# RWKV-style attention, routed experts and a dense layer on one core: loads of 48 rows, and the attention's pieces from one written list

## The chip, the core and the metric

The kernel runs on one core of a Trainium2 chip. The metric is the device time of one execution in microseconds (us), as a median of several runs; lower is better. The core has five engines with queues of their own: PE (matrix products, with the weight loads PEld as a second row of the profile), DVE (vector), ACT (scalar), POOL (GpSimd) and SP, which here only issues transfers. Transfers run on 16 DMA engines that all queues share.

## The reference

Three layers follow each other. The first is a linear attention with a state of 40x40 for each of 4x8 heads, over 768 steps; the second sends each of the 3072 tokens to one of 8 experts; the third is a dense layer with an exponential activation.

```python
for t in range(S):                      # S = 768, per (batch, head)
    y[:, :, t] = np.einsum('bhd,bhde->bhe', rt, state)
    Sa = np.einsum('bhde,bhe->bhd', state, at)
    state = state * wt[:, :, None, :] - np.einsum('bhd,bhe->bhde', Sa, bt) + np.einsum('bhd,bhe->bhde', vt, kt)
...
logits = x @ w_gate; expert_idx = np.argmax(logits, axis=1)      # x: 3072 x 320
h = np.maximum(disp @ w1, 0.0); y = h @ w2                       # 8 experts, 320 -> 1024 -> 320
out[i] = gate_w[i] * y[expert_idx[i], pos[i]]
...
h = x @ w_in; g = np.where(h > 0, h, np.exp(np.minimum(h, 0)) - 1); return g @ w_out   # 320 -> 2048 -> 320
```

## The kernel before

**Units.** The 768 steps are cut into 12 chunks of 64. A unit is one chunk of 16 of the 32 heads, so there are 24 units, u = 0 to 23; units of one parity follow each other through the state, so the work is two interleaved recurrences. A unit's 16 heads lie as 8 pairs on two halves of the partitions: rows 0 to 39 and 64 to 103 hold the 40 channels.

**Steps of a unit.** Each step is a generator whose `yield` stands where another engine takes over, and has a letter. `e`/`E` loads the unit's decays, a, k and b (from `in_e`, two transfers of 40 rows x 2058 words; `e` on SP in two halves for the first ten units, `E` on the ACT queue later), `d` loads r and v (`in_d`, two transfers of 40 rows), `v` loads v by token. `p` makes running decays and scales a, k, b on DVE (L243 to L255). `a` copies a on ACT, `c` is the score product on PE (L277), its eviction on ACT and the store of the scores to a DRAM scratch `dab`; `m` masks them (L295), `k` transposes k and b (L304, L306). `l` brings a piece of `dab` back with one small system a partition; `i` solves those systems on POOL by 31 steps of two instructions (L351, L353), for a group of units at once: groups 0 and 1 are units 0, 1 and 2, 3, and groups 2 to 6 are four units each. `o` stores the solution (`dx`), `t` loads it for one unit, `f`/`g` join small inverses to one of 64 (PE L433 and L444, DVE L426). Then the recurrence: `r` (PE L459), `u` (L469, ACT L471), `w` (L479), `s` (L494, DVE L503, L504), `h`, and beside it the outputs `q` (L525, DVE L530), `z` and `y` (L539, L552, DVE L556) and `x` (L562, ACT L567, DVE L569), which gives token rows and their logits. `b`, `j` and `D` route the rows and scatter them into the expert buffers (POOL L610). `V` are pieces of DVE work that split the dense layer's weights ahead of time, and a further generator loads and splits the first expert's weights.

**What sets the order.** Every engine runs its instructions in the order in which the program gives them out. That order is a list of step names: each name runs its step to its next `yield`. Before, the first part is written out as text (`ORDER`), up to the first pieces of the slot of unit 5, and the rest is made by `slot(k)` for k = 5 to 24 from one pattern. A name stands in the list as often as its step has pieces; `q15.1` is the second half of `q` of unit 15.

**After the attention** the expert blocks and then the dense layer run on PE, with everything else beside it.

Of the kernel before, what the change touches and what calls it, by code (L numbers as in the profile page):

```python
# [33 lines left out]
ORDER = """
se1 sa0 se0 se0 v1 sc0 e0.0 sv se1 e0.1 sd p0 sw p0 e1.0 sw a0 p0 v0 p1 sa1 sx a0 p1 lw sz st1 e2.0 c0.0 a1
p2 p2 a1 c0.0 e1.1 sr1 Z7 c0.1 p1 e3.0 c0.1 k0.0 k0.1 c0.1 c1.0 e2.1 a2 a2 c1.0 p3 c1.1 k1.1 k1.0 c1.1 k1.0 e4.0 d1 k1.1
c1.1 e3.1 m0.0 l0 m0.1 k0.1 p2 p3 a3 l1 a3 p4 p4 p3 m1.1 c2.1 e5.0 k2.1 c2.0 c2.1 m1.0 r0 c2.0 k2.0 k0.0 a4 m2.1 a4 p5
st0 k2.0 k3.1 sc1 c3.0 c2.1 c3.1 ss1 k3.0 e4.1 m2.0 p4 r0 r1 c4.0 i0 e6.0 k3.0 n0 k3.1 m3.0 k4.1 p5 n1 o0 c3.1 p6
c3.0 e5.1 a5 a5 c3.1 m3.1 k2.1 r1 e7.0 l2 p5 k4.1 c4.1 k4.0 m4.1 e6.1 c4.0 c5.1 k5.1 l3 p6 k5.0 c5.0 c4.1 p7 c4.1 p6 a6
m5.0 a6 v2 v3 p7 c5.0 t1 m4.0 t0 c6.1 m6.1 c5.1 k4.0 f1 k6.1 c5.1 k6.0 k6.1 m5.1 sr0 a7 i1 c6.0 f1 f0 a7 o1 e7.1 e8.0 f1 f0  # L40
k5.0 p7 c6.1 f0 f1 f1 p8 c6.0 d0 e9.0 f0 k5.1 c7.1 f0 f1 f1 c6.1 c7.0 f0 f0 e8.1 c7.1 g1 c7.0 g0 p8 m7.0 a8 ss0 p8 m7.1
g0 k7.1 l5 l4 g1 k7.0 k7.1 g0 k8.0 g0 c7.1 l6 p9 e9.1 g1 a8 u0 m6.0 p9 k6.0 k8.1 u0 g1 l7 c8.0 k7.0 m8.0 c8.1 n2 t2 e10
w0 a9 p9 f2 n3 k8.1 a9 q0.0 w0 q0.1 q0.1 w0 i2 u1 u1 f2 q0.0 c8.0 f2 p10 k9.1 c9.1 f2 c8.1 c9.0 m8.1 k8.0 Z2 c8.1 f2 w0
Z4 p10 t3 f2 s0 k9.1 p10 c9.1 c9.0 w1 w1 k9.0 y0 f2 i2 k9.0 g2 s0 w1 e11 s0 c9.1 f3 k10.1 Z3 r2 a10 w1 a10 f3 k10.1 m9.0
f3 y0 m9.1 k10.0 p11 Z0 r2 c10.0 q1.0 q1.0 c10.1 x0 f3 p11 h2 q1.1 s1 f3 g2 a11 k10.0 m10.1 i2 f3 c10.0 g2 q1.1 c10.1 h2
e12 v4 p11 f3 s1 c10.1 x0 y1 y1 d2 g3 p12 a11 s1 k11.1 c11.0 x1 g3 r3 Z6 c11.0 g2 g3 p12 k11.1 h3 x1 m11.0 a12 Z5 p12 x0 r3
u2 a12 c11.1 c12.0 u2 g3 w2 d3 c11.1 w2 k11.0 w2 x1 k12.1 h3 q2.0 q2.1 Z1 b0 w2 c11.1 c12.1 u3 c12.1 m10.0 m11.1 s2 j0
o2 u3 w3 k11.0 q2.1 q3.1 c12.0 e13 z2 q2.0 s2 w3 y2 s2 l11 j0 l10 y2 t4 m12.0 m12.1 r4 v5 l9 g4 d4 w3 k12.1 r4 p13 D0
h4 x2 l8 g4 c12.1 k12.0 D1 h4 t5 q3.0 p13 w3 g4 g4 g4 s3 u4 x2 a13 l12 s3 z3 q3.0 u4 w4 w4 a13 q3.1 p13 i3 w4 g5 h5 y3
d5 x2 w4 y3 s3 s4 i3 k12.0 e14 t6 s4 s4 h5 v6  # L50
"""
FIRST = [f for f, n in GROUPS if f > 6]
AHEAD = (17, 19, 20, 21, 22, 23)

CV0, CVN = 17, 7


def slot(k):
    L = []
    a = lambda x: L.extend(x.split())  # L60
    live = k < NU

    nx, up = k + 1, k + (8 if k < 7 else 9)
    ups = up < NU
    pair = k - 3 if k % 2 else None
    work = {f - 6 + i: (g, i) for g, (f, n) in enumerate(GROUPS) for i in range(4) if f > 8}
    work[5] = (3, 3)
    w = work.get(k)
    if live: a(f"r{k} r{k}")
    if ups and k != 7: a(f"c{up}.0")  # L70
    if FU <= k < NU: a(f"g{k} g{k}")
    more = ups and up + 1 < NU
    if ups and k != 7: a(f"m{up}.0 c{up}.0")
    if more and k != 7: a(f"p{up+1}")
    a(f"x{k-2} x{k-2} x{k-2}")
    if k == NU: a(f"b{NU-2}.1")
    if FU <= k < NU: a(f"g{k} g{k}")
    if w and w[1]:
        a(f"i{w[0]}")
        if w[1] == 3: a(f"o{w[0]}")  # L80
    if k % 2 == 0: a(f"D{k-3}")
    second = f"c{up}.1 m{up}.1 c{up}.1 c{up}.1 p{up+1} l{up}"
    if ups: a(second if k != 7 else f"a{up} a{up} c{up}.0 m{up}.0 c{up}.0 p{up+1}")
    if k + 2 < NU: a(f"v{k+2}")
    V = (lambda: a("V")) if CV0 <= k < NU else (lambda: None)

    if nx in FIRST: a(f"t{nx}")
    a(f"q{k-1}.0 q{k-1}.0")
    V()
    if w and not w[1] and k != 6: a(f"i{w[0]}")  # L90
    if live: a(f"u{k} u{k}")
    if k == 7: a(second)
    if more: a(f"p{up+1}")
    a(f"q{k-1}.1 q{k-1}.1")
    V()
    if pair is not None: a(f"b{pair}")
    if ups:
        a(f"k{up}.0 k{up}.0 k{up}.1 k{up}.1")
    if FU <= nx < NU and nx not in FIRST: a(f"g{nx}")
    if live and k < 22: a(f"w{k} w{k} w{k} w{k}")  # L100
    if up + 2 < NU: a(f"E{up+2}")
    if more: a(f"a{up+1} a{up+1}")
    a(f"z{k-1}")
    if nx < NU: a(f"h{nx} h{nx}")
    if nx < NU: a(f"d{nx}")
    if k + 2 < NU and k + 2 not in FIRST: a(f"t{k+2}")
    if live and k < 22: a(f"s{k} s{k} s{k}")
    if k == NU: a(f"j{NU-2}.1 j{NU-2}.1 D{NU-2}")
    a(f"y{k-1} y{k-1}")
    if nx in FIRST: a(f"g{nx}")  # L110
    V()
    if pair is not None: a(f"j{pair} j{pair} D{pair}")
    if k == 6:
        up += 1
        a(f"c{up}.0 m{up}.0 c{up}.0 c{up}.1 m{up}.1 c{up}.1 c{up}.1 p{up+1} l{up} i{w[0]}")
        a(f"k{up}.0 k{up}.0 k{up}.1 k{up}.1 E{up+2} p{up+1} p{up+1}")
    return " ".join(L)


def attention(tc, nc, e_in, v_tok, d_in, wg, disp, xt, cst, ring, early, early_w, cv, cap):  # L120
# [548 lines left out]
    for k in range(KR, NU + 1):
        for key in slot(k).split():  # L670
            go(key)
        for _ in range(AHEAD.count(k)):
            next(early, None)
        if k == 8:
            zero_x()
# [813 lines left out]
```

## Time and profile before

| | |
|---|---|
| median of 3 runs | 1049.46 us (1043.61 to 1050.21) |
| time of the profiled execution | 1050.7 us |
| its span, first to last instruction | 1049.0 us |
| mean granted clock of PE | 0.946 |
| busy: PE, DVE, POOL, ACT | 963.1, 726.2, 614.4, 514.5 us |

A time on a row counts from the span's start. "Idle before, releaser" in brackets is the time for which the engine stood still ahead of the row, and what ended it. The granted clock (PEclk) is a share of full speed; in the trace it stands at 0.5 or at 1.0, and a stretch shows the mean. The DMA share is the mean busy share of the 16 DMA engines.

### The profile page before, as it was taken

How to read it: one execution, taken by the hardware profiler on the slowest of the kernel's cores; microseconds unless marked ns; L12 is line 12 of the kernel's file. 1: busy time of each engine (PE TensorE's matmuls, PEld its weight loads, DVE VectorE, ACT ScalarE, POOL GpSimd, SP SyncE). 2: the span in 40 equal slices, each digit the busy share in tenths (PEclk: the TensorE clock that was granted, in tenths of full speed). 3: DMA queues.
4: the chain of work that ended last, by engine and by line, in shares of the span. 5: the costliest groups of instructions: out<-in, count | busy, mean ns of one | idle time of the engine just before them, and what ended most of it. 6: DMA issues, size and time to landing. Idle time of an engine off the chain costs nothing.

```text
span 1049.0 us, 25349 instructions
## 1 busy us (share of the span) xinstructions
PE 963.1 (92%) x9995; PEld 868.3 (83%) x9995; DVE 726.2 (69%) x1287; ACT 514.5 (49%) x1011; POOL 614.4 (59%) x926
## 2 busy tenths in 40 slices
PE   4869988898899999989999999999999999999993
PEld 4858877798888888778988888889889988998893
DVE  8955857888674567649888963676667667676761
ACT  4646544556363334254445456464555555554551
POOL 4767839899898803377777776744333334333342
PEclk9866989899899889999999999999999999999997
DMA  6768776667555585376877764501001010100000
GB/s 169 163 175 185 179 138 117 150 136 140 129 118 115 126 199 117 120 215 202 258 225 213 216 201 149 199 23 26 26 1 45 7 26 26 26 26 1 26 1 28
DMA packets 180984, 121.67 MB, mean 116 GB/s; under 512 B 105792, under 2 KB 166872, under 8 KB 179224
## 3 DMA queue, kind: packets, MB, share of 16 engines
q1 hardware_dynamic: 176788, 102.89, 39.5%
q0 software_dynamic: 3168, 11.14, 3.0%
q10 hardware_dynamic: 900, 5.93, 2.2%
q8 instruction: 81, 1.33, 0.6%
q14 instruction: 47, 0.39, 0.1%
HBM read 86.87 MB, written 33.05 MB: 114 GB/s over the span
## 4 chain that ended last, share of the span: by engine, by line
PE 41%; DVE 7%; issue 3%; DMA 3%; ACT 2%; POOL 1%; SPq 0%; POOLq 0%; ACTq 0%; DVEq 0%
PE ph L968 21%; PE po L994 5%; PE po L993 5%; PE po L992 5%; DVE L L1098 1%; DMA w<-E 1%; ACT X L1091 1%; DVE E L859 1%; DVE N L864 1%; PE po L1037 1%; PE po L1039 1%; DMA xt<-Y 1%; DMA ring<-in_w_dram 1%; PE po L1038 1%; PE po L1033 1%
## 5 line engine op out<-in xcount | busy, mean ns | idle before, releaser
L780 POOL TENSOR_TENSOR ring<-ring,ring 128x64 fp32r<-128x64 f32 (+2 forms) x320 | 197.0, 656 | 83.9 <-ACT ring L775 83.9
L1112 POOL TENSOR_TENSOR L<-E,H 128x512 fp32r<-128x512 f32 x66 | 94.3, 1429 | 166.6 <-ACT H L1111 154.4
L968 PE MATMUL ph<-XH,ring 128*128 128x512 f32 (+1 forms) x640 | 170.7, 388 | 0.9 <-ACT XH L952 0.5
L1105 ACT ACTIVATE E<-N 128x512 f32<-128x512 f32 x96 | 60.8, 633 | 155.1 <-POOL L L1112 78.0
L968 PEld LDWEIGHTS ph<-XH,ring 128*128 128x128 f32 x640 | 115.7, 189 | 15.3 <-ACT XH L952 0.9
L353 POOL TENSOR_TENSOR X<-X,ring 128x60 f32<-128x60 f32 (+19 forms) x170 | 115.6, 680 | 13.3
L994 PE MATMUL po<-ring,L 128*128 128x320 f32 x384 | 119.4, 311 | 1.5 <-POOL L L1112 1.5
L992 PE MATMUL po<-ring,H 128*128 128x320 f32 x384 | 118.5, 309 | 0.4 <-ACT H L1111 0.4
L993 PE MATMUL po<-ring,H 128*128 128x320 f32 x384 | 118.5, 309 | 0.0
L968 PE MATMUL ph<-XS,ring 128*128 128x512 f32 (+1 forms) x320 | 97.1, 384 | 0.0
L968 PE MATMUL ph<-XL,ring 128*128 128x512 f32 (+1 forms) x320 | 96.9, 384 | 0.0
L351 POOL TENSOR_TENSOR ring<-X,ring 128x60 f32<-128x60 f32 (+19 forms) x108 | 73.8, 683 | 37.2 <-DMA ring<-dab 16.6
L1104 DVE TENSOR_SCALAR N<-ph 128x512 f32<-128x512 f32 x96 | 65.7, 685 | 33.2 <-PE ph L968 33.0
L1109 DVE SCALAR_TENSOR_TENSOR M<-E,M 128x512 f32<-128x512 f32 x96 | 72.6, 756 | 14.5 <-ACT M L1106 14.5
L992 PEld LDWEIGHTS po<-ring,H 128*128 128x128 f32 x384 | 72.1, 188 | 4.8 <-ACT H L1111 0.6
L993 PEld LDWEIGHTS po<-ring,H 128*128 128x128 f32 x384 | 72.1, 188 | 4.3
L994 PEld LDWEIGHTS po<-ring,L 128*128 128x128 f32 x384 | 72.2, 188 | 2.0 <-POOL L L1112 2.0
L1110 DVE SCALAR_TENSOR_TENSOR E<-ph,M 128x512 f32<-128x512 f32 x96 | 66.4, 692 | 7.8
L968 PEld LDWEIGHTS ph<-XL,ring 128*128 128x128 f32 x320 | 60.9, 190 | 11.1
L968 PEld LDWEIGHTS ph<-XS,ring 128*128 128x128 f32 x320 | 60.1, 188 | 10.8 <-DVE XS L953 0.4
L775 ACT CAST ring<-ring 128x704 fp32r<-128x704 f32 x80 | 61.4, 779 | 13.7 <-PE po L1039 6.8
L1111 ACT CAST H<-E 128x512 fp32r<-128x512 f32 x96 | 59.0, 614 | 11.0 <-DVE E L1110 7.8
(238 smaller groups left out, 2162.9 us busy)
## 6 DMA issues: line engine op xcount, KB each, us to landing
ring<-in_w_dram SPq DMA_DIRECT2D x16, 640.0 KB
ring<-in_w_dram SPq DMA_DIRECT2D x32, 256.0 KB
RVU<-in_d_in_dram SPq DMA_DIRECT2D x48, 160.0 KB
dab<-AB SPq DMA_DIRECT2D x24, 256.0 KB
ring<-in_e_in_dram ACTq DMA_DIRECT2D x18, 321.6 KB
ring<-w SPq DMA_DIRECT2D x4, 1408.0 KB
disp<-ring SPq DMA_DIRECT2D x8, 575.8 KB
...
```

The lines of the kernel that those rows point to most:

```text
L351: nc.gpsimd.tensor_tensor(tv, X[:, 0:n, s:s + 1].to_broadcast([128, n, m]), N[:, s:s + 1, s + 1:e].to_broadcast([128, n, m]), op=ALU.mult)
L353: nc.gpsimd.tensor_tensor(X[:, 0:n, s + 1:e], X[:, 0:n, s + 1:e], tv, op=ALU.subtract)
L775: s.nc.scalar.copy(B[:, 0:704], r)
L780: s.nc.gpsimd.tensor_tensor(B[:, to], r[:, q], B[:, q].bitcast(F32), op=ALU.subtract)
L968: nc.tensor.matmul(p, l, r[:, 0:s.T], start=i == 0, stop=i == len(seq) - 1)
L992: nc.tensor.matmul(o, H[:, c], hb, start=f == 0, stop=False)
L993: nc.tensor.matmul(o, H[:, c], lb, start=False, stop=False)
L994: nc.tensor.matmul(o, L[:, c], hb, start=False, stop=f == s.W.nf - 1)
L1104: nc.vector.tensor_scalar(N, p, 0.0, None, op0=ALU.min)
L1109: nc.vector.scalar_tensor_tensor(out=M, in0=E, scalar=1.0, in1=M, op0=ALU.add, op1=ALU.mult)
L1110: nc.vector.scalar_tensor_tensor(out=E, in0=p, scalar=0.0, in1=M, op0=ALU.max, op1=ALU.add)
L1112: eng.tensor_tensor(L, E, H.bitcast(F32), op=ALU.subtract)
```

## The change

Three things change. (1) The loads `e`, `E` and `d` move 48 rows in place of 40: the host pads each half by eight rows (decays of one, the rest zero), which land on partitions 40 to 47 and 104 to 111. (2) `slot` is gone, and one written list gives out all pieces of the 24 units; it holds the same 1335 names as before, and 72 of them stand elsewhere. Two new names are no steps: `A` takes the next piece of the first expert's weights and `X` clears a row of the token buffer, both where the loop did it before. (3) For the last unit alone the logits (L569) are given out ahead of the ACT copy of its token rows.

```diff
@@ load_e
-            eng.dma_start(out=t[64 * hp:64 * hp + 40, c], in_=e_in[u, hp, :, c])
+            eng.dma_start(out=t[64 * hp:64 * hp + 48, c], in_=e_in[u, hp, :, c])
@@ load_d
-            nc.sync.dma_start(out=RVU[u % 2][64 * bp:64 * bp + 40, :, bp:3:2 - bp], in_=d_in[u, bp])
+            nc.sync.dma_start(out=RVU[u % 2][64 * bp:64 * bp + 48, :, bp:3:2 - bp], in_=d_in[u, bp])
@@ x_out
+        logits = lambda: nc.vector.tensor_reduce(cst["lg"][:, u, 1:9], pv[:, :, 80:88].rearrange("p j e -> p e j"), axis=AX.X, op=ALU.add)
+        if u == NU - 1:
+            logits()
         nc.scalar.copy(XO[:, 0:D].rearrange("p (j x) -> p j x", j=4), pv[:, :, 0:80])
         yield
-        nc.vector.tensor_reduce(cst["lg"][:, u, 1:9], pv[:, :, 80:88].rearrange("p j e -> p e j"), axis=AX.X, op=ALU.add)
+        if u < NU - 1:
+            logits()
@@ ORDER
...
+y3 s3 s4 i3 k12.0 e14 s4 s4 h5 v6 r5 r5 c13.0 x3 g5 t6 g5 m13.0 c13.0 p14 x3 x3 c13.1 g5 g5 i3 o3 m13.1 c13.1 c13.1 p14 l13 v7 q4.0 q4.0 u5 u5 p14
...
+h23 V j20 j20 h23 D20 A x22 x22 x22 b22.1 D21 q23.0 q23.0 q23.1 q23.1 z23 y23 y23 j22.1 j22.1 D22
@@ go
+        if key == "A":
+            next(early, None)
+            return
@@ host_layout
+    pad = np.zeros((24, 2, 8, 2058), np.float32)
+    pad[..., 0:520] = 1
+    pad[..., 0:520:65] = 0
...
+    return np.concatenate([out, pad], 2), v_tok, np.concatenate([d_in, np.zeros_like(d_in[:, :, 0:8])], 2)
```

**Place 1: SP, the loads that feed the first solve of four units.** `LM` holds group 2's systems; `dab_556`, `dab_587`, `dab_805` and `dab_904` (`dab_901` in the change) are the scores of units 4, 5, 6 and 7, and `ring_91` is the buffer of the odd units' `e` loads. Before:

```order
L330 DMA LM_106<-dab_587 16x32x32 x2
L330 DMA LM_106<-dab_556 16x32x32 x2
L291 DMA dab_904<-AB 64x1024
L330 DMA LM_106<-dab_805 16x32x32 x2
L230 DMA ring_91<-in_e_in_dram 40x1024 x2
L330 DMA LM_106<-dab_904 16x32x32 x2
L365 DMA TA<-dab_401 64x8x64 x2
```

And with the change:

```order
L286 DMA LM_106<-dab_587 16x32x32 x2
L286 DMA LM_106<-dab_556 16x32x32 x2
L286 DMA LM_106<-dab_805 16x32x32 x2
L247 DMA dab_901<-AB 64x1024
L186 DMA ring_91<-in_e_in_dram 48x1024 x2
L286 DMA LM_106<-dab_901 16x32x32 x2
L321 DMA TA<-dab_500 64x8x64 x2
```

The load of unit 6's systems goes ahead of the store of unit 7's scores; the `e` load stays between that store and the load that reads it back.

**Place 2: PE, the start of the slot of unit 5.** `xp` and `t_...` are the two products of `g`, `x` is the token product of unit 3, `sc` the scores of unit 13. Before:

```order
L459 MATMUL rhs<-VS_138,AM_132 64x40 x16
L277 MATMUL sc<-ring_91 128x128 x4
L433 MATMUL xp<-AB,TA 32x32 x16
L562 MATMUL x<-IW,XT 128x88 x4
L444 MATMUL t_2151<-TT_122,TA 32x32 x16
L277 MATMUL sc<-ring_91 128x128 x4
```

And with the change:

```order
L415 MATMUL rhs<-VS_138,AM_132 64x40 x16
L233 MATMUL sc<-ring_91 128x128 x4
L518 MATMUL x<-IW,XT 128x88 x4
L389 MATMUL xp<-AB,TA 32x32 x16
L233 MATMUL sc<-ring_91 128x128 x4
L400 MATMUL t_2156<-TT_122,TA 32x32 x16
```

The token product now stands ahead of the first product of `g`, and the second half of the scores ahead of its second; unit 6 has the same two moves.

**Place 3: PE, the end of the attention.** `y` and `x` belong to unit 23, `rt` counts the rows of unit 22 and then of unit 23. Before:

```order
L539 MATMUL y<-RVU_120,SD_141 64x128 x8
L597 LDWEIGHTS tri
L597 MATMUL rt<-roh,tri 128x8
L598 LDWEIGHTS ones
L598 MATMUL rt<-ACC,ones 128x8
L552 MATMUL y<-Qs,KB_109 64x64 x16
L562 MATMUL x<-IW,XT 128x88 x4
L634 MATMUL warm<-ring_5566 128x512 x6
```

And with the change:

```order
L495 MATMUL y<-RVU_120,SD_141 64x128 x8
L508 MATMUL y<-Qs,KB_109 64x64 x16
L557 LDWEIGHTS tri
L557 MATMUL rt<-roh,tri 128x8
L558 LDWEIGHTS ones
L558 MATMUL rt<-ACC,ones 128x8
L518 MATMUL x<-IW,XT 128x88 x4
L594 MATMUL warm<-ring_5567 128x512 x6
```

Unit 23's output product stands ahead of the counting of unit 22.

## Rows read from the trace of the kernel before

**Rows 1.** Busy time by stage: stretch, length, engines (instructions), granted clock, DMA.

```profile
0.00:60.00 60.00, 35.20 (x288) 33.86 (x288) 46.84 (x84) 30.61 (x62) 38.61 (x91) 0.90 0.66 164
60.00:143.00 83.00, 72.43 (x1474) 67.26 (x1474) 55.42 (x93) 43.94 (x99) 55.45 (x92) 0.76 0.77 180
143.00:278.00 135.00, 120.64 (x2180) 110.12 (x2180) 103.47 (x185) 72.79 (x158) 113.11 (x160) 0.91 0.67 137
278.00:444.00 166.00, 155.07 (x2985) 140.60 (x2986) 109.58 (x267) 65.18 (x150) 98.17 (x158) 0.93 0.55 128
444.00:1049.00 605.00, 579.78 (x3070) 516.46 (x3068) 410.89 (x662) 301.96 (x542) 309.08 (x428) 0.99 0.31 94
```

**Rows 2.** Waits of PE, 140 to 445 us: total, times, longest.

```profile
PE vu L479 <- ACT RVU L471: 7.8, 5, 4.0
PE xp L433 <- DVE AB L426: 6.3, 2, 3.2
PE sc L277 <- ACT ring L264: 2.7, 1, 2.7
```

**Rows 3.** POOL in order of time: first instruction of solves 0, 2, 3; a store.

```profile
30.18 0.34 POOL L351 TENSOR_TENSOR ring<-X,ring 128x15 f32<-128x15 f32 x1 [16.55 <-DMA ring<-dab]
...
82.56 0.23 POOL L351 TENSOR_TENSOR ring<-X,LM 128x31 f32<-128x31 f32 x1 [11.43 <-DMA TA<-dab]
...
151.89 0.23 POOL L351 TENSOR_TENSOR ring<-X,ring 128x31 f32<-128x31 f32 x1 [12.17 <-DMA dab<-AB]
...
264.06 0.61 POOL L359 DMA_DIRECT2D dx<-X  x1 [0.30 <-POOL X L353]
```

**Rows 4.** The page: ACT's DMA queue (packets, MB, share); its issues (number, size).

```profile
q10 hardware_dynamic: 900, 5.93, 2.2%
...
ring<-in_e_in_dram ACTq DMA_DIRECT2D x18, 321.6 KB
```

**Rows 5.** Who waited for the E loads (us, times).

```profile
  DVE ring L243: 16.0, 11
  DVE ring L255: 4.3, 3
```

**Rows 6.** DVE and SP in order of time, ahead of solve 2.

```profile
64.88 1.25 DVE L255 TENSOR_TENSOR ring<-ring 104x1024 f32<-104x1024 f32 x1 [3.17 <-DMA ring<-in_e_in_dram]
...
72.36 0.50 SPq L291 DMA_DIRECT2D dab<-AB  x1
...
77.10 0.68 SPq L230 DMA_DIRECT2D ring<-in_e_in_dram  x2
77.88 0.86 SPq L330 DMA_DIRECT2D LM<-dab  x2
```

**Rows 7.** SP in order of time, between solves 2 and 3.

```profile
130.10 0.37 SPq L359 DMA_DIRECT2D dx<-X  x1
130.57 0.95 SPq L230 DMA_DIRECT2D ring<-in_e_in_dram  x2
...
134.70 4.59 SPq L379 DMA_DIRECT2D TA<-dx  x1
...
146.79 1.02 SPq L330 DMA_DIRECT2D ring<-dab  x2
```

**Rows 8.** DVE in order of time, unit 12's first use of solve 4.

```profile
277.74 0.70 DVE L426 STREAM_TRANSPOSE AB<-TA 32x512 f32<-32x512 f32 x1 [3.23 <-DMA TA<-dx]
```

**Rows 9.** The end of the attention: DVE, and POOL's last scatter, in order of time.

```profile
440.67 0.19 DVE L569 TENSOR_REDUCE LG<-x 128x8 f32<-128x32 f32 x1 [1.68 <-ACT XO L567]
...
443.57 0.96 POOL L610 DMA_INDIRECT disp<-XO,SLOT  x1 [3.68 <-issue]
```

**Rows 10.** PE in order of time: what moved products take, and the last token product.

```profile
195.72 1.12 PE L562 MATMUL x<-IW,XT 128*128 128x88 f32 x8
...
274.31 1.16 PE L277 MATMUL sc<-ring 128*128 128x128 f32 x8
...
439.05 1.12 PE L562 MATMUL x<-IW,XT 128*128 128x88 f32 x8 [0.79 <-DVE XT L556]
```

More of the change, by code (lines that the diff above doesn't have):

```diff
@@ L39 @@
[L39 to L48, printed above, removed]
@@ L49 @@
-h4 x2 l8 g4 c12.1 k12.0 D1 h4 t5 q3.0 p13 w3 g4 g4 g4 s3 u4 x2 a13 l12 s3 z3 q3.0 u4 w4 w4 a13 q3.1 p13 i3 w4 g5 h5 y3
-d5 x2 w4 y3 s3 s4 i3 k12.0 e14 t6 s4 s4 h5 v6
-"""
[L52 to L117, printed above, removed]
@@ new lines @@
+se1 sa0 se0 se0 v1 sc0 e0.0 sv se1 e0.1 sd p0 sw p0 e1.0 a0 p0 v0 p1 sa1 sx a0 p1 sw lw sz st1 e2.0 c0.0 a1 p2 p2 a1 c0.0 e1.1 sr1 Z7 c0.1 p1 e3.0
+c0.1 k0.0 k0.1 c0.1 e2.1 a2 a2 p3 c1.1 c1.0 c1.0 k1.1 k1.0 c1.1 k1.0 e4.0 d1 k1.1 c1.1 e3.1 m0.0 l0 m0.1 k0.1 p2 p3 a3 l1 a3 p4 p4 p3 m1.1 c2.1 e5.0
+k2.1 c2.0 c2.1 m1.0 r0 c2.0 k2.0 k0.0 a4 m2.1 a4 p5 st0 k2.0 k3.1 sc1 c3.0 c2.1 c3.1 ss1 k3.0 e4.1 m2.0 r1 p4 c4.0 r0 i0 e6.0 k3.0 n0 k3.1 m3.0 p5 n1
+o0 c3.1 p6 c3.0 e5.1 a5 a5 c3.1 m3.1 k2.1 r1 e7.0 l2 p5 k4.1 k4.1 c4.1 k4.0 m4.1 e6.1 c4.0 c5.1 k5.1 l3 p6 k5.0 c5.0 c4.1 p7 c4.1 p6 a6 m5.0 a6 v2 v3
@@ new lines @@
+p17 v9 t8 q6.0 q6.0 u7 u7 c16.1 m16.1 c16.1 c16.1 p17 l16 p17 q6.1 q6.1 b4 k16.0 k16.0 k16.1 k16.1 w7 w7 w7 w7 E18 a17 a17 z6 h8 h8 d8 t9 s7 s7 s7 y6
+y6 g8 j4 j4 D4 r8 r8 c17.0 g8 g8 m17.0 c17.0 p18 x6 x6 x6 g8 g8 i4 D5 c17.1 m17.1 c17.1 c17.1 p18 l17 v10 q7.0 q7.0 u8 u8 p18 q7.1 q7.1 k17.0 k17.0
+k17.1 k17.1 g9 w8 w8 w8 w8 E19 a18 a18 z7 d9 h9 h9 t10 s8 s8 s8 y7 y7 X r9 r9 c18.0 g9 g9 m18.0 c18.0 p19 x7 x7 x7 g9 g9 i4 o4 c18.1 m18.1 c18.1 c18.1
+p19 l18 v11 q8.0 q8.0 u9 u9 p19 q8.1 q8.1 b6 k18.0 k18.0 k18.1 k18.1 g10 w9 w9 z8 w9 w9 E20 a19 a19 h10 h10 d10 t11 s9 s9 s9 y8 y8 j6 j6 D6 r10 r10
@@ new lines @@
+q14.1 q14.1 b12 w15 w15 z14 w15 w15 s15 h16 h16 d16 t17 s15 s15 y14 y14 g16 j12 j12 D12 r16 r16 g16 g16 x14 x14 x14 g16 g16 k23.0 i6 D13 v18 q15.0
+q15.0 u16 u16 q15.1 q15.1 g17 w16 w16 w16 w16 z15 d17 t18 s16 h17 h17 s16 s16 y15 y15 r17 r17 g17 g17 x15 x15 x15 g17 g17 i6 o6 q16.0 q16.0 V V u17
+u17 q16.1 q16.1 b14 g18 v19 w17 w17 w17 w17 z16 h18 h18 d18 t19 s17 s17 s17 y16 y16 V j14 j14 D14 A r18 r18 g18 g18 x16 V x16 x16 g18 g18 D15 v20
+q17.0 q17.0 u18 q17.1 q17.1 V g19 u18 w18 w18 z17 w18 w18 h19 d19 s18 s18 s18 y17 y17 V r19 r19 g19 g19 x17 x17 x17 g19 g19 v21 t20 q18.0 q18.0 V u19
@@ new lines @@
+u19 q18.1 q18.1 V b16 w19 w19 w19 w19 z18 d20 t21 s19 h20 h20 s19 s19 y18 y18 g20 V j16 j16 D16 D17 A r20 r20 g20 g20 x18 x18 x18 h19 g20 g20 v22
+q19.0 q19.0 V V u20 u20 q19.1 q19.1 g21 w20 w20 w20 w20 h21 z19 h21 d21 t22 s20 s20 s20 y19 y19 V V A r21 r21 g21 g21 x19 x19 x19 g21 g21 v23 q20.0
+q20.0 u21 u21 q20.1 q20.1 V b18 g22 w21 w21 w21 w21 z20 h22 h22 d22 t23 s21 s21 s21 y20 y20 V j18 j18 D18 A r22 r22 g22 g22 x20 x20 x20 g22 g22 D19
+q21.0 q21.0 V u22 u22 q21.1 q21.1 V g23 z21 d23 y21 y21 V A r23 r23 g23 g23 x21 x21 x21 g23 g23 q22.0 q22.0 V u23 u23 q22.1 q22.1 V b20 z22 y22 y22
@@ L120, in attention @@
+h23 V j20 j20 h23 D20 A x22 x22 x22 b22.1 D21 q23.0 q23.0 q23.1 q23.1 z23 y23 y23 j22.1 j22.1 D22
+"""
+CVN = 7
 def attention(tc, nc, e_in, v_tok, d_in, wg, disp, xt, cst, ring, early, early_w, cv, cap):
@@ L637, in attention @@
                  n=m_load, t=tt_load, f=t32, g=t64, r=rhs, u=u_solve, w=vu_tr, s=s_update, h=s_tr, q=q_mm, z=y_state, y=y_mm, x=x_out,
-                 b=route, j=route_mm, D=scatter, Z=zero_d, V=lambda: cv.pieces(spare, CVN))
+                 b=route, j=route_mm, D=scatter, Z=zero_d, X=zero_x, V=lambda: cv.pieces(spare, CVN))
     def spare(i, words):
@@ L668, in attention @@
         go(key)
[L669 to L675, printed above, removed]
     for _ in early:
@@ L1449, in d_side @@
         return np.ascontiguousarray(y.transpose(3, 0, 1, 5, 2, 4)).reshape(24, 2, 40, 8, 64)
-    return out, v_tok, np.stack([d_side(r), d_side(v)], 4)
+    pad = np.zeros((24, 2, 8, 2058), np.float32)
+    pad[..., 0:520] = 1
+    pad[..., 0:520:65] = 0
+    d_in = np.stack([d_side(r), d_side(v)], 4)
+    return np.concatenate([out, pad], 2), v_tok, np.concatenate([d_in, np.zeros_like(d_in[:, :, 0:8])], 2)
 def network(tc, nc, e_in, v_tok, d_in, wg, cap, w1, w2, w_in, w_out, out):
```

24 lines of the change are left out of this document (19 added, 5 removed).

## The prediction, made before the result was known

> **What bounds the kernel now.** I read the busy times by stage first. From 444 us on nothing of the change is left: the experts and the dense layer take 605 us, PE is busy for 579.8 of them at a granted clock of 0.99, and no instruction there is moved [rows 1]. So only the attention, 0 to 444 us, can change. Its stages differ. Up to 60 us PE is busy for 35 of 60 us and DVE for 47: the start is a chain of loads, preparation and first scores. From 60 to 143 us PE is busier (72 of 83) but at a mean clock of 0.76, and from 143 to 444 us it is busy for 120.6 of 135 and 155.1 of 166 us at 0.91 and 0.93. The DMA engines are busiest where the start is decided: a mean share of 0.66 and 0.77 up to 143 us, 0.67 and 0.55 after.
>
> Then I read POOL in order of time, because its solves are one long series and each waits for transfers at its start. Solve 0 starts at 30.18 us after 16.55 us of waiting, solve 2 at 82.56 after 11.43, solve 3 at 151.89 after 12.17 [rows 3]. Behind that point POOL hardly stops: solve 4 is stored at 264.06 us, and POOL is busy for 113.1 us of the stretch from 143 to 278, of which 8.9 us lie ahead of solve 3 [rows 1, 3]. At 277.74 us DVE takes up unit 12, the first of solve 4, after 3.23 us of waiting for a load of that solution [rows 8]. So up to unit 12 the pace is that of the solves: what PE alone gains between 143 and 278 us it gives back there, and what lets solves 2 and 3 start earlier is kept. Behind unit 12 PE and the recurrence decide; PE stands still there for 166 - 155.1 = 10.9 us [rows 1].
>
> **The loads of 48 rows.** What they do to a transfer has to be bounded, since no load of 48 rows is in this trace. The ACT queue carries nothing but 18 E loads, two for each of nine units: 900 packets for 18 issues are 50 each, 40 rows and ten more [rows 4]. I read the ten as one closing packet for each DMA engine that takes part: ten engines with four rows each. 48 rows divide into 16 engines with three each. A load would then move a fifth more bytes, but its fullest engine would carry a quarter less, and the ten engines that all E and d loads share would be relieved by a quarter of that traffic.
>
> [...]
>
> What it is worth is read from the waits. DVE waits for E loads 11 times for 16.0 us and three times for 4.3 us [rows 5]; most of these stand where DVE is not the last to arrive, so the total is an upper bound only. The ones on the way to a solve count.
>
> *Ahead of solve 2* the way is: the second half of unit 7's E load, for which DVE waits 3.17 us until 64.88; its scores, stored at 72.36; the load that reads them back, issued at 77.88; solve 2 at 82.56 [rows 3, 6]. The wait of 3.17 us could go wholly or not at all. I take half, 1.5 us, because the load's own travel shrinks by at most a quarter while the queueing behind other loads shrinks with it. For the read-back, 82.56 - 77.88 = 4.7 us, I take 0.5 us of less crowding. Together 2.0 us, between 0 and 4.4 (the whole wait and a quarter of the read-back).
>
> *Ahead of solve 3* there are 151.89 - 130.10 = 21.8 us between the store of solve 2 and the first step of solve 3, nearly all transfers: the store, with a full E load issued 0.5 us behind it, the first load of the result, which holds SP's queue for 4.59 us from 134.70, and behind it in that queue the last scores' load, issued at 146.79, 5.1 us before the solve [rows 3, 7]. A quarter off all of it would be 5.4 us; but most of these transfers use other shapes and only share the engines. I take 1.5 us, between 0 and 5.4.
>
> PE's wait of 2.7 us for an ACT copy of a [rows 2] has an E load behind it, but it lies ahead of unit 12, where solve 4 sets the pace; it only helps PE to keep up. I count 0. The d loads' extra rows cost SP nothing, since the number of issues stays.
>
> **The list.** 72 names stand elsewhere and none is new, so no engine has more work; only who waits changes. At the first place SP gives out the read-back of unit 6 ahead of unit 7's store. Nothing is bought by it: solve 2 needs unit 7's read-back, and that stays behind an E load that holds the queue until 77.10 [rows 6]. At the second place x (1.12 us on PE) goes ahead of g's first product and half of the scores (1.16 us) ahead of its second [rows 10], in the slots of units 5 and 6. That brings scores forward by about a microsecond and puts the unit's inverse back by 2.3. It lies ahead of unit 12; I count 0, between -4.6 (both units, wholly on the recurrence) and +2. For the moves behind unit 12 (pieces of V, of y, of z between the two halves of w) the most that can be filled is the 10.9 us for which PE stands still [rows 1]; the longest named waits of PE, 7.8 us for the eviction of u and 6.3 us for DVE's turn in g [rows 2], have their causes on ACT, DVE and in loads, not in the list's order around them. I take 2.0 us, between -3 and +7.
>
> *The end of the attention* is a plain chain. The last token product starts at 439.05 and takes 1.12 us, so it ends at 440.17; the logits start at 440.67, after waiting for ACT's copy, and the last scatter at 443.57 [rows 9, 10]. Given out first, the logits start 0.5 us earlier, and with the third place's move y no longer waits for the counting of unit 22, some 0.1 us. I take 0.6 us. ACT's copy then waits for the logits, but only the scatter needs it, nearly three microseconds later.
>
> **The sum.** 2.0 + 1.5 + 2.0 + 0.6 = 6.1 us less than the profiled execution's 1050.7 us (span 1049.0 and 1.7 around it): 1044.6 us. That execution was 1.2 us over the median of the runs, 1049.46, so the median after should be near **1043 us**, 0.6% less. Differences under 1% are about what a measurement of this kernel can't tell from no change.
>
> **The rivals.**
> *The loads carry more than I grant them.* If the ten shared engines are what holds up nearly everything before 278 us, the waits for E loads go nearly in full at the places that count and the scores come back faster as well. Price: half of the 20.3 us of DVE waits [rows 5], plus a quarter of the 11.43 and 12.17 us that POOL waits ahead of solves 2 and 3 [rows 3], 5.9 us, plus the list and the end as above, 2.6 us: 10.2 + 5.9 + 2.6 = 18.7 us, about 1031 us. For it speaks the DMA share of 0.77 as a mean over 16 engines: if ten carry more than the rest, those are near full. Against it: POOL would have to start each solve 5 to 10 us earlier, and DVE, busy for 47 of the first 60 us, has little room there.
> *Hidden anyway.* Solve 2's start hangs on SP's order and on PE's clock (0.76 in that stage), not on how long a load travels, and the moves cancel. Then only the end's 0.6 us is left: 1049 us.
> *The recurrence is put back.* The pieces set ahead of g and of w's second half (x and scores in the slots of units 5 and 6, 2.3 us each; z, of about the length of x, 1.1 us, ahead of w's second half in four slots) stand on the way from one state to the next of the same parity. If that way, and not PE's load or the solves, sets a slot's length, each delays all that follows: 4.6 + 4.4 = 9.0 us, and against the loads' 3.5 and the end's 0.6 us the kernel is 4.9 us slower, about 1054 us; if the other moves do the same it reaches 1061. It decides from the point where ACT's and DVE's evictions, not PE, end last in a slot. For it speaks the 7.8 us of PE waiting for u's eviction [rows 2]; against it that PE is busy for 93% of the time behind unit 12.
>
> **How the numbers follow.** The forecast, 3 to 10 us less, has 0.47. The larger gain, 11 to 24 us, has 0.32: the terms' upper ends add to 17.9 us with the end. Hidden anyway (within 3 us of before) has 0.11. The recurrence put back has 0.10, of which half stays within 1% (10.5 us). So faster by over 1% is 0.32, within 1% is 0.63, slower by over 1% is 0.05. The range runs from 1028 (most of the larger gain) to 1054 (the smaller price of the slower case).
>
> **What would show it.** The ACT queue's packets should be 18 x 64 = 1152 in place of 900. Solve 2 should start near 80.5 us and solve 3 near 148; the waits of DVE for E loads should fall below 14 us in total; unit 12's first use should be near 274, the logits' reduction should follow the last token product with no ACT copy between, and the last scatter should start near 437.5. The stretch behind it should still take 605 us. If solve 3 starts below 144 us, the larger gain is at work; if it starts where it did, and the end has moved, the list did it; if the starts have moved and the last scatter has not, the recurrence took the gain back.

## The result and the profile after

The changed kernel takes 1062.72 us (median of 6 runs, 1054.22 to 1067.07) against 1049.84 us of the kernel before beside it: a ratio of 1.013, interval 1.0094 to 1.0166. It is 12.9 us slower; the forecast was 1043. The profiled execution took 1067.07 us, with a span of 1065.4 us, 16.4 us more than before; it is the slowest of the six. Beside it stands a second profile of the same kernel, from the run `after2` below: 1058.39 us, the fastest of another six. Single profiles of one kernel differ by several us, so the readings that carry the argument are given from both.

Lines that were there before have numbers lower by 40 to 46, most by 44 (solves L351 are now L307, E loads L230 are L186, scans L243 are L199, logits L569 are L523, scatters L610 are L570).

Busy time by stage in the kernel after, columns as in [rows 1]; the last stretch begins at its last scatter:

```profile
0.00:60.00 60.00, 37.66 (x288) 36.41 (x288) 46.66 (x83) 30.06 (x62) 35.18 (x79) 0.86 0.82 171
60.00:143.00 83.00, 66.83 (x1464) 61.60 (x1465) 53.27 (x92) 43.65 (x98) 56.66 (x101) 0.84 0.92 190
143.00:278.00 135.00, 114.88 (x2069) 106.19 (x2067) 100.29 (x175) 69.75 (x152) 105.78 (x148) 0.90 0.90 144
278.00:456.80 178.80, 164.07 (x3110) 149.92 (x3110) 115.21 (x277) 69.80 (x159) 103.09 (x174) 0.90 0.64 133
456.80:1065.40 608.60, 584.13 (x3072) 519.75 (x3070) 417.30 (x663) 303.49 (x542) 303.58 (x428) 0.98 0.32 94
```

The column before the last has moved most. The mean share of the DMA engines was 0.66, 0.77 and 0.67 up to 278 us [rows 1] and is 0.82, 0.92 and 0.90, while the GB/s behind it rose by 4 to 6% only. So the engines are held longer for nearly the same data.

ACT's DMA queue, which carries E loads alone, on the page of the kernel after (packets, MB, share):

```profile
q10 hardware_dynamic: 1152, 7.11, 3.6%
```

The packets are the 18 x 64 that were forecast. In the trace 864 of them are rows of 8232 bytes and 288 are closing packets of four bytes, sixteen a load; before it was 720 and 180, ten a load. Before, most often ten rows of this queue are in flight at once (23.3 of the 45.8 us in which any are), after most often sixteen (18.7 of 51.0 us), so closing packets are counted as engines here. SP's queue has 588 more packets of four bytes than before (11512, not 10924), which is 6 x 98, and it issues 50 E loads and 48 d loads. But for 20% more bytes than in [rows 4] the queue takes 3.6% of sixteen engines' span, not 2.2%: 0.036 x 16 x 1065.4 = 614 us of engine time against 0.022 x 16 x 1049.0 = 369. Over 864 and 720 rows of data that is 0.71 us a row against 0.51.

POOL after, in order of time: the first instructions of solves 0, 2 and 3, the stores of solve 4 and of the last solve. They answer to [rows 3].

```profile
33.95 0.22 POOL L307 TENSOR_TENSOR ring<-X,ring 128x15 f32<-128x15 f32 x1 [20.93 <-DMA ring<-dab]
...
88.71 1.63 POOL L307 TENSOR_TENSOR ring<-X,LM 128x31 f32<-128x31 f32 x1 [14.53 <-DMA TA<-dab]
...
157.93 0.23 POOL L307 TENSOR_TENSOR ring<-X,ring 128x31 f32<-128x31 f32 x1 [13.21 <-DMA dab<-AB]
...
269.46 0.61 POOL L315 DMA_DIRECT2D dx<-X  x1 [0.30 <-POOL X L309]
...
378.61 0.61 POOL L315 DMA_DIRECT2D dx<-X  x1 [0.30 <-POOL X L309]
```

Solve 0 is late by 3.8 us, solve 2 by 6.1, solve 3 by 6.0, the store of solve 4 by 5.4. (Solve 0 alone says little: in the first experiment below it starts at 32.9 us, and nothing is lost.) The last solve was stored at 365.83 us before:

```profile
365.83 0.61 POOL L359 DMA_DIRECT2D dx<-X  x1 [0.30 <-DVE rt L602]
```

It is now 12.8 us late. In the second profile solves 2 and 3 start, and the last solve is stored, at:

```profile
86.70 0.23 POOL L307 TENSOR_TENSOR ring<-X,LM 128x31 f32<-128x31 f32 x1 [12.93 <-DMA TA<-dab]
...
159.72 0.46 POOL L307 TENSOR_TENSOR ring<-X,ring 128x31 f32<-128x31 f32 x1 [8.89 <-DMA dab<-AB]
...
377.58 0.61 POOL L315 DMA_DIRECT2D dx<-X  x1 [0.30 <-DVE XO L530]
```

That is 4.1, 7.8 and 11.8 us late. Where this is lost shows in POOL's waits in the first 445 us after (in total, times, longest):

```profile
POOL X L298 <- DMA dx<-X: 5.9, 3, 2.1
...
POOL ring L307 <- DMA VS<-in_v_tok_dram: 4.7, 1, 4.7
```

POOL waits for its own store to be through before it may clear X, and for loads that stand ahead of its next solve; before, these two were 0.3 and 0.5 us in all. (In the second profile they are 5.1 and 4.9 us, the latter put down to the read-back of the systems.) The solves themselves are no slower: from solve 4's first instruction to its store it is 55.6 us before and 55.0 after. Who waited for the E loads after (as [rows 5]):

```profile
  DVE ring L199: 23.7, 14
  DVE ring L211: 3.5, 2
```

The scans waited 23.7 us where it had been 16.0, and DVE's two waits for E together 27.2 us in place of 20.3; in the second profile they are 17.1 and 21.7. Ahead of solve 2, DVE and then SP after, in order of time (as [rows 6]):

```profile
67.97 1.23 DVE L211 TENSOR_TENSOR ring<-ring 104x1024 f32<-104x1024 f32 x1 [2.41 <-DMA ring<-in_e_in_dram]
...
77.29 0.81 SPq L247 DMA_DIRECT2D dab<-AB  x1
81.53 0.79 SPq L186 DMA_DIRECT2D ring<-in_e_in_dram  x2
82.41 0.91 SPq L286 DMA_DIRECT2D LM<-dab  x2
```

Unit 7's second half is taken up 3.1 us late, its scores are stored 4.9 us late, and from the issue of their read-back to solve 2 it is 88.71 - 82.41 = 6.3 us in place of 4.7. Between solves 2 and 3, SP after (as [rows 7]):

```profile
137.03 0.36 SPq L315 DMA_DIRECT2D dx<-X  x1
137.49 1.45 SPq L186 DMA_DIRECT2D ring<-in_e_in_dram  x2
...
141.03 3.69 SPq L335 DMA_DIRECT2D TA<-dx  x1
```

From that store to solve 3 it is 20.9 us, against 21.8 before: nothing is lost here in this execution. Unit 12's first use of solve 4 and the end of the attention, DVE and POOL after (as [rows 8, 9]):

```profile
288.21 0.70 DVE L382 STREAM_TRANSPOSE AB<-TA 32x512 f32<-32x512 f32 x1 [5.27 <-DMA TA<-dx]
...
453.87 0.19 DVE L523 TENSOR_REDUCE LG<-x 128x8 f32<-128x32 f32 x1 [0.66 <-PE x L518]
...
456.80 0.97 POOL L570 DMA_INDIRECT disp<-XO,SLOT  x1 [1.82 <-issue]
```

Unit 12 is 10.5 us late and the last scatter 13.2 us. The 608.6 us behind it are 3.2 us more than the 605.4 of before, in a part that the change doesn't touch; in the other profiles of this study it is 603.0 to 609.1 us.

### The profile page after: what moved, and what is told of

The parts are those of the page before. It is cut to its first block, busy times and chain, and to the rows that moved or that the text cites. A ratio compares the mean times of both kernels' runs of the same rounds, so it can differ in the third digit from the quotient of the medians.

```text
span 1065.4 us, 25347 instructions
## 1 busy us (share of the span) xinstructions
PE 967.6 (91%) x9995; PEld 873.9 (82%) x9995; DVE 732.7 (69%) x1287; ACT 516.7 (49%) x1011; POOL 604.3 (57%) x926
## 3 DMA queue, kind: packets, MB, share of 16 engines
q10 hardware_dynamic: 1152, 7.11, 3.6%
## 4 chain that ended last, share of the span: by engine, by line
PE 27%; issue 11%; DVE 6%; POOL 6%; DMA 4%; ACT 2%; SPq 1%; POOLq 0%; DVEq 0%; ACTq 0%
PE ph L924 14%; PE po L950 3%; PE po L949 3%; PE po L948 3%; POOL L L1068 3%; DMA ring<-in_w_dram 2%; DMA w<-E 2%; POOL ring L736 1%; DVE L L1054 1%; POOL out_dram L1239 1%; DVE E L815 1%; DVE N L820 1%; SPq L757 1%; ACT ring L731 1%; DVE M L821 1%
## 5 line engine op out<-in xcount | busy, mean ns | idle before, releaser
L1068 POOL TENSOR_TENSOR L<-E,H 128x512 fp32r<-128x512 f32 x66 | 88.2, 1337 | 172.8 <-ACT H L1067 161.7
L309 POOL TENSOR_TENSOR X<-X,ring 128x60 f32<-128x60 f32 (+19 forms) x170 | 123.3, 726 | 13.3
L924 PEld LDWEIGHTS ph<-XH,ring 128*128 128x128 f32 x640 | 115.7, 189 | 16.4 <-DVE L L1054 1.4
L307 POOL TENSOR_TENSOR ring<-X,ring 128x60 f32<-128x60 f32 (+19 forms) x108 | 69.3, 641 | 46.8 <-DMA ring<-dab 20.9
L1065 DVE SCALAR_TENSOR_TENSOR M<-E,M 128x512 f32<-128x512 f32 x96 | 75.8, 789 | 10.7 <-ACT M L1062 10.6
L950 PEld LDWEIGHTS po<-ring,L 128*128 128x128 f32 x384 | 72.9, 190 | 2.0 <-POOL L L1068 2.0
L924 PEld LDWEIGHTS ph<-XS,ring 128*128 128x128 f32 x320 | 60.4, 189 | 10.7 <-DVE XS L909 0.3
L481 PE MATMUL q<-RVU 128*128 128x128 f32 x384 | 63.3, 319 | 3.2 <-issue 3.2
```

The costliest lines, as they stand in the source:

```text
L307: nc.gpsimd.tensor_tensor(tv, X[:, 0:n, s:s + 1].to_broadcast([128, n, m]), N[:, s:s + 1, s + 1:e].to_broadcast([128, n, m]), op=ALU.mult)
L309: nc.gpsimd.tensor_tensor(X[:, 0:n, s + 1:e], X[:, 0:n, s + 1:e], tv, op=ALU.subtract)
L924: nc.tensor.matmul(p, l, r[:, 0:s.T], start=i == 0, stop=i == len(seq) - 1)
L950: nc.tensor.matmul(o, L[:, c], hb, start=False, stop=f == s.W.nf - 1)
L1065: nc.vector.scalar_tensor_tensor(out=M, in0=E, scalar=1.0, in1=M, op0=ALU.add, op1=ALU.mult)
L1068: eng.tensor_tensor(L, E, H.bitcast(F32), op=ALU.subtract)
```

## The experiments

A figure used throughout: **us a row** is the share of ACT's queue, times 16 engines, times the span, over 18 x the rows of a load. The share is printed to 0.1%, so it is known to about 0.012 us. The expectations for 32 + 8, 40 + 8, 52 and 64 rows still divide by all packets, closing ones included: their 0.41 and 0.53 us for 40 and 48 rows are 0.51 and 0.70 us a row here.

**Which part?** Theory L: the loads of 48 rows cost the time. Theory O: the written order does. The changed kernel with loads of 40 rows (list and logits stay):

```diff
-            eng.dma_start(out=t[64 * hp:64 * hp + 48, c], in_=e_in[u, hp, :, c])
+            eng.dma_start(out=t[64 * hp:64 * hp + 40, c], in_=e_in[u, hp, 0:40, c])
@@ load_d: 40 rows in the same way
```

> The changed kernel with loads of 40 rows again; list and logits stay as changed. Theory L (the loads of 48 rows cost the time: the DMA share before 278 us rose from about 0.7 to 0.9 with them): between 1040 and 1050 us, so 0 to 10 us under the kernel before, with DMA shares as before, solve 2 near 82 us and solve 3 near 151. Theory O (the written order costs it, by putting the recurrence back): 1058 to 1066 us, with the DMA shares of before.

Measured: 1046.99 us, ratio 0.9995 (0.996 to 1.003). The list and the logits change nothing that can be measured. Next the kernel before with 48 rows in E and d, in E alone, and in d alone (the same lines, edited in the kernel before):

> The kernel before with loads of 48 rows alone; its order and logits stay. Theory L: 1060 to 1070 us, DMA share about 0.8 to 0.9 up to 278 us, solve 2 near 88 us and solve 3 near 158. Theory O: 1043 to 1051 us.

> The kernel before with 48 rows in the E loads alone. Theory L with the E loads as cause (8 KB rows, 1.0 ms of DMA engine time before): nearly all of what 48 rows cost, 1058 to 1068 us. Theory O: 1044 to 1051 us.

> The kernel before with 48 rows in the d loads alone (768 pieces of 256 bytes a load in place of 640). Theory L with the E loads as cause: 1047 to 1053 us. If the small pieces of the d loads are the cause: 1057 to 1066 us. Theory O: 1045 to 1052 us.

Measured: 1.0175 (1.0103 to 1.0246), 1.0077 (1.0036 to 1.0118) and 1.0017 (0.9974 to 1.006). Theory L holds, O falls: E's rows by themselves bring a loss, though less than both loads together, and d's by themselves none that can be measured (up to 0.6%). The padded arrays lie in DRAM in the list's kernel with 40 rows too, so it is the rows moved that cost. The last solve's store, with 48 rows in E alone and in d alone:

```profile
376.48 0.61 POOL L359 DMA_DIRECT2D dx<-X  x1 [0.30 <-POOL X L353]
```

```profile
366.81 0.61 POOL L359 DMA_DIRECT2D dx<-X  x1 [0.30 <-POOL X L353]
```

10.7 us late and 1.0 us late.

**Bytes, or how the rows are shared?** Two kernels split each E load in two issues, 32 + 8 rows (the bytes of before) and 40 + 8:

```diff
-            eng.dma_start(out=t[64 * hp:64 * hp + 40, c], in_=e_in[u, hp, :, c])
+            for r in (slice(0, 32), slice(32, 40)):
+                eng.dma_start(out=t[64 * hp + r.start:64 * hp + r.stop, c], in_=e_in[u, hp, r, c])
```

> The kernel before with each E load issued as two, rows 0 to 31 and rows 32 to 39: the bytes of before, but a load of 32 rows can be shared by all sixteen DMA engines and every E load is issued twice. Theory B (the loads of 48 rows cost what their added rows carry, 20% more): no slower than before, ratio 0.995 to 1.005, and the queue of ACT takes per row what it took before, 2.2% of sixteen engines' span over 900 rows, 0.41 us. Theory S (the spread over sixteen engines costs, whatever the bytes): as slow as the 48 rows in E alone, ratio 1.005 to 1.013, and 0.5 us or more per row on ACT's queue.

> The kernel before with E of 48 rows, loaded as 40 rows and 8 rows: the bytes of 48 rows, but five sixths of them go as they went before. Theory B: as slow as 48 rows in one load, ratio 1.005 to 1.013. Theory S: ratio 0.999 to 1.005, and per row on ACT's queue under 0.47 us, against 0.53 us of the 48 rows in one.

Measured: 1.0201 (1.0134 to 1.0269) and 1.0277 (1.0209 to 1.0345), more than either theory allowed. So a control was made, split 20 + 20, which leaves ten engines:

> The kernel before with each E load issued as two of 20 rows: the bytes and the ten engines of before, two rows to an engine and a load; the control for the two kernels with doubled issues, which were 2.0% and 2.8% slower. If the doubled issues cost that, this one is slower by 1.5 to 3% as well, and those two tell nothing of how rows are shared; if the sharing did, its ratio is 0.997 to 1.005.

Measured: 1.0247 (1.0195 to 1.03). With the issues doubled and ten engines kept the kernel is already 2.5% slower, so the times of these three kernels tell nothing of the sharing; that a load of 32 rows was shared by sixteen engines isn't shown either; what the packets of the control tell stands behind the table below. The better way is a single load with another number of rows, padded by the host as the change does:

```diff
-            eng.dma_start(out=t[64 * hp:64 * hp + 40, c], in_=e_in[u, hp, :, c])
+            eng.dma_start(out=t[64 * hp:64 * hp + 52, c], in_=e_in[u, hp, :, c])
@@ host_layout
+    pad = np.zeros((24, 2, 12, 2058), np.float32)
+    pad[..., 0:520] = 1
+    pad[..., 0:520:65] = 0
```

> The kernel before with E loads of 52 rows, which can be shared by thirteen engines of four rows each: 30% more bytes than before. Theory B: slower than with 48 rows, by one and a half of its 8 us, ratio 1.008 to 1.017, with a price per row as with 40. Theory S: spread over more engines than ten and fewer than sixteen, ratio 1.003 to 1.008; the price per row on ACT's queue lies between 0.41 and 0.53 us, and if what costs is three rows to an engine instead of four it is 0.41 to 0.44 us.

> The kernel before with E loads of 64 rows, sixteen engines of four rows each: 60% more bytes than before. Theory B: three times the cost of 48 rows, ratio 1.018 to 1.03, price per row on ACT's queue 0.41 us. Theory S: the price per row is that of 48 rows, 0.5 us or more, and the ratio 1.015 to 1.04; if three rows to an engine are what costs, per row 0.41 to 0.44 us and the ratio below 1.012.

> The kernel before with E loads of 42 rows, which can be shared by fourteen engines of three rows each: 5% more bytes than before. A price per row is the share of ACT's queue in the sixteen engines' span, spread over the rows of data alone: 0.51 us with 40 rows, 0.70 with 48, 0.56 with 52 and with 64. [...] Theory N (the price goes with the number of engines that load at once): 0.55 to 0.58. Theory B (bytes): 0.51, ratio 1.000 to 1.003.

> The kernel before with E loads of 44 rows, eleven engines of four rows each: 10% more bytes than before, twice what 42 rows add. [...] Theory N: 0.52 to 0.55. Theory B: 0.51, ratio 1.002 to 1.006, above that of 42 rows.

> The kernel before with E loads of 50 rows, ten engines of five rows each: 25% more bytes than before, no engine more. [...] Theory N: 0.51 a row. Theory B: 0.51 a row, ratio 1.008 to 1.014.

> The kernel before with E loads of 45 rows, fifteen engines of three rows each: 12.5% more bytes, half of what 50 rows add, and the dear form of sharing. All theories that are left: 0.64 to 0.72 us a row, so the loads of ACT's queue take 520 to 580 us of the engines in all, against 476 with 50 rows. Theory B (what the time goes by is the rows added): ratio 1.002 to 1.006, and DVE waits 15 to 19 us for E at its first scans. Theory T (it goes by the time that the rows take of the engines): ratio 1.007 to 1.011, DVE waits over 20 us.

All of them, with the kernel before and the 48 rows in E alone:

| rows of a load | engines x rows | rows added | us a row | engine time of ACT's queue, us | ratio (interval) | last solve stored at, us |
|---|---|---|---|---|---|---|
| 40 (before) | 10 x 4 | 0 | 0.51 | 369 | 1 | 365.8 |
| 42 | 14 x 3 | 5% | 0.65 | 488 | 1.0047 (1.0012 to 1.0083) | 370.3 |
| 44 | 11 x 4 | 10% | 0.57 | 451 | 1.0025 (0.9998 to 1.0052) | 365.5 |
| 45 | 15 x 3 | 12.5% | 0.67 | 541 | 1.0048 (1.0013 to 1.0082) | 368.9 |
| 48 | 16 x 3 | 20% | 0.70 | 609 | 1.0077 (1.0036 to 1.0118) | 376.5 |
| 50 | 10 x 5 | 25% | 0.53 | 476 | 1.0090 (1.0058 to 1.0123) | 376.9 |
| 52 | 13 x 4 | 30% | 0.56 | 522 | 1.0101 (1.0036 to 1.0166) | 371.2 |
| 64 | 16 x 4 | 60% | 0.56 | 643 | 1.0130 (1.0094 to 1.0167) | 380.6 |

Each ratio is against the kernel before run beside it. The last column is of one execution each, and that with 44 rows was the fastest of its twelve (1046.7 us), so it is a rough guide only.

The column of the engines is read from the packets: ACT's queue on the pages with 45 and with 50 rows:

```profile
q10 hardware_dynamic: 1080, 6.67, 3.2%
```

```profile
q10 hardware_dynamic: 1080, 7.41, 2.8%
```

1080 packets over 18 loads are 60: 45 + 15, and 50 + 10. The 50 rows are more data and take less of the engines.

On the price of a row the case holds that the expectations for 52 and 64 rows set apart, that three rows to an engine are what costs (by all packets a row is 0.45 us with 52 and with 64 rows, where they had 0.41 to 0.44): 0.65 to 0.70 us wherever an engine has three rows, 0.51 to 0.57 where it has four or five, whether ten engines load or sixteen. (The 0.57 of 44 rows lies above what N and B gave.) Theory N falls (16 x 4 costs 0.56, 14 x 3 costs 0.65), and so do B's constant 0.51 a row and S, where it had the spread itself as the price. The closing packets are not the price either, although rows by three have more of them: by the packets of the traces they take 0.02 to 0.03 us each, and split 20 + 20, a load has one for every two rows, and a row costs 0.023 x 16 x 1067.9 / 720 = 0.55 us.

On the time neither T nor B, as the expectation for 45 rows puts them, holds throughout. Against T: with 50 rows an engine's row is as quick as before and no engine is added, yet the kernel is 0.9% slower; with 45 rows the queue takes 541 us of the engines, not 476, and the kernel is 0.5% slower. From 44 to 52 rows the loss is 0.025 to 0.04% for each percent of rows added, as B has it. Against B: 42 rows add 5% and cost 0.47%, where B had at most 0.3%; 64 rows add 60% and cost 1.3%, where B had 1.8% or more. Nor does the fullest engine's share order the losses: 4 x 0.57 = 2.3 us with 44 rows, 4 x 0.56 = 2.2 with 64. But the intervals of 45 and 50 rows overlap, so the part that the dear rows have in the time isn't settled by the times.

How long a load travels can be worked out from the starts and durations of ACT's packets in the traces: from the first packet of a unit's two loads to the end of the last it is, as the median of the nine units, 4.9 to 5.3 us in three profiles with 40 rows, 5.1 to 5.9 in six with 48, and 6.3 with 50. So loads of 48 rows hold more engines and are through no sooner; loads of 50 rows hold an engine hardly longer for a row and are through about a microsecond later. Two shapes lose, and perhaps in two ways.

A rival that no run takes out is the clock of PE. The mean granted clock of the executions is 0.945 before, 0.943 with 44 rows, 0.940 with 42, 0.938 with 48 in E alone and 0.940 with 50, and a lower one goes with longer executions of one and the same kernel (before, beside the 45 rows: 1042.2 us at 0.954, 1055.3 us at 0.938). How much of a loss is waiting and how much is clock, and whether the waits bring the lower clock, wasn't taken apart.

**Whose E loads?** 48 rows only in the E loads that ACT issues, for the last nine units:

```diff
+            rows = 48 if eng is nc.scalar else 40
-            eng.dma_start(out=t[64 * hp:64 * hp + 48, c], in_=e_in[u, hp, :, c])
+            eng.dma_start(out=t[64 * hp:64 * hp + rows, c], in_=e_in[u, hp, 0:rows, c])
```

> The kernel before with 48 rows only in the E loads that ACT issues (the last nine units), 40 in those that SP issues. If each E load that lands later delays its own unit, the nine of 24 units have some 3 to 4 us of the 8: ratio 1.002 to 1.005, and the first 143 us are as before. If the loss comes of SP's queue, on which the solves' reloads stand behind the E loads, this kernel is as fast as before: 0.998 to 1.001.

Measured: 1.0051 (1.0019 to 1.0084), the stages up to 143 us as before. The last nine of 24 units carry their part of the loss or more, so it isn't bound to SP's queue. In the trace it shows at one place, POOL's first instruction of the last solve. Before and with these nine units padded:

```profile
323.84 0.29 POOL L351 TENSOR_TENSOR ring<-X,ring 128x31 f32<-128x31 f32 x1 [0.51 <-DMA VS<-in_v_tok_dram]
```

```profile
327.62 0.48 POOL L352 TENSOR_TENSOR ring<-X,ring 128x31 f32<-128x31 f32 x1 [5.56 <-DMA VS<-in_v_tok_dram]
```

Solve 4 had been stored only 0.7 us late. Unit 23, whose E load is the last of all, begins its first scan 2.3 us late (299.96 us, not 297.65) and its last score product 5.3 us late (318.69, not 313.41), and the last solve needs those scores. The same wait is 5.3 us with 42 rows, 7.0 with 45, 5.7 with 48, 5.0 with 50 and 52, 1.9 with 44 and 1.8 with 64 (which had lost its time earlier), and 1.2 in the changed kernel with loads of 40. That it is this wait which lengthens the kernel isn't shown: in the profiled execution, 2.5 us under the median, the last scatter is where it was before (443.8 us, 443.6).

**Do d's rows cost on top of E's?** The changed kernel with d loads of 40 rows, and the changed kernel again beside it:

> The changed kernel with d loads of 40 rows again: E loads of 48 rows, the written list and the logits stay. Theory D (the d rows cost on top of E's, though alone they cost nothing): ratio 1.004 to 1.010, and at least 0.4% less than the changed kernel beside it. Theory N (E's rows are the whole loss): ratio 1.010 to 1.016, within 0.3% of the changed kernel.

> The changed kernel once more, beside the one with d loads of 40 rows on the same chip. Theories D and N both: ratio 1.010 to 1.016.

Measured: 1.0069 (1.004 to 1.0097) and 1.0136 (1.0095 to 1.0177). Theory D holds, as far as it says that d's rows cost on top of E's: they are about half of the loss, some 5 us by the medians (1060.04 against 1054.96) or 7 by the ratios. That they cost more there than alone isn't shown: alone it was 0.17%, between -0.26 and 0.6%, on top it is 0.67 points, and the intervals leave room for one and the same cost. The stretch from 143 to 278 us, with d's 48 rows alone, with E's (and the list), and with both:

```profile
143.00:278.00 135.00, 120.72 (x2180) 110.70 (x2180) 102.59 (x184) 73.01 (x158) 111.28 (x155) 0.90 0.73 140
```

```profile
143.00:278.00 135.00, 119.28 (x2175) 109.70 (x2173) 103.04 (x185) 73.46 (x159) 109.35 (x157) 0.92 0.80 145
```

```profile
143.00:278.00 135.00, 121.61 (x2208) 112.14 (x2206) 105.28 (x187) 73.13 (x160) 105.01 (x147) 0.91 0.90 148
```

The DMA share goes 0.67 before, 0.73, 0.80, 0.90, and the last solve is stored at 365.8, 366.8, 373.4 and 377.6 us. That crowded engines let a transfer cost what it hadn't cost before fits these four. It doesn't fit the loads of 50 rows, where the share in this stretch is hardly above that of before while the last solve is 11.1 us late:

```profile
143.00:278.00 135.00, 113.39 (x2067) 103.61 (x2066) 101.32 (x179) 69.70 (x153) 103.62 (x146) 0.91 0.69 141
```

So crowding is a reading, not shown to be the cause; what each single transfer loses wasn't taken apart. No version tried beats the kernel before.

## Why the prediction was wrong

**What bounds the kernel** was right: from 444 us on nothing changed beyond the spread of the profiles, and the kernels with a clear loss store the last solve late. How far a late solve reaches the end is loose: from the last solve's store to the last scatter it is 77.7 us before, 78.2 after, 72.9 in the second profile after and 68.7 in the changed kernel with loads of 40 rows, whose granted clock from 278 to 444 us is 0.97 against 0.93 before.

**The loads of 48 rows** is the step that failed, and in its sign. It said that a load "would then move a fifth more bytes, but its fullest engine would carry a quarter less", and from this took 2.0 and 1.5 us off, with bounds that ended at nothing. Sixteen engines with three rows each was right (1152 packets). That a row costs the same on each of them was not: 3 rows x 0.71 us = 2.1 us, and before 4 x 0.51 = 2.05. The fullest engine carries no less time, a unit's loads pass no sooner (5.1 us before, 5.1 to 5.9 with 48 rows), the other six engines carry as much, and all of them together are held 1.66 times as long, in stages where the rows had already shown shares of 0.55 to 0.77. Solve 2 came at 88.7 us (86.7 in the second profile), not 80.5, solve 3 at 157.9 (159.7), not 148, and DVE's waits for E rose from 20.3 to 27.2 us in total (21.7), where under 14 were forecast. How the rows added become 8 us of the kernel's time with E alone, by the engines' time, by later landings or by PE's clock, stays open. A row that asked for a bound on the other side was there: a load spread over more engines holds engines that other transfers may want, and [rows 1] shows how few were idle; from 143 to 278 us the share went from 0.67 to 0.90. A bound on the side of loss, of the added fifth alone, would have been 0.2 x 369 = 74 us of engine time on ACT's queue; it was 245.

How many engines take part in a load is read from its packets in each run: 10 for 40 rows, 14 for 42, 11 for 44, 15 for 45, 16 for 48, 10 for 50, 13 for 52, 16 for 64. The number gives no price of a row. That E and d loads share the same ten engines was an assumption of the prediction; the packets in the trace have no engine's number, so no run shows it.

Why rows by three are dear the trace doesn't show, since it doesn't tell which row goes to which engine. By the number of rows to an engine only three was dear: 0.55 us a row with two to an engine (20 + 20), 0.65 to 0.71 with three, 0.51 to 0.57 with four, 0.53 with five.

**d's loads** were counted with E's. Alone they cost nothing that can be measured; on top of E they cost some 5 to 7 us, a term that the prediction didn't have. It counted their issues on SP, and each of these even became shorter (830 to 637 ns, below).

**The list** (2.0 us, bounds -3 to +7) and **the end** (0.6 us) are measured together by the changed kernel with loads of 40 rows: from 0.996 to 1.003 of 1048.46 us, between a gain of 4.2 and a loss of 3.1 us. Their 2.6 us lie within, and so does nothing. The logits do follow the last token product directly (453.87 us, after PE). Of the list's 1335 names 1328 are those of before and seven are `A` and `X`.

**The rivals.** *The recurrence is put back* named times near the result (1054 to 1061 us), by a mechanism that isn't there: the same order with loads of 40 rows is as fast as before. PE's waits after, from 140 to 465 us (as [rows 2]):

```profile
PE xp L389 <- DVE AB L382: 11.9, 3, 6.5
...
PE sc L233 <- ACT ring L220: 3.0, 1, 3.0
...
PE vu L435 <- ACT RVU L427: 0.8, 2, 0.5
```

The wait for u's eviction, which that rival rested on, is nearly gone (2.0 us in the second profile, from 140 to 465 us). The wait for the small inverses has doubled here, and behind it is a load of the solution, but not in the second profile:

```profile
PE xp L389 <- DVE AB L382: 5.0, 2, 4.7
```

*Hidden anyway* and *the loads carry more* fall with the step on the loads. The upper ends that were set against the larger gain add to 4.4 + 5.4 + 7 + 0.6 = 17.4 us, not 17.9; the forecast doesn't rest on it.
